# Expert lists from masks of an expert's ten usual blocks, made for five tiles at a time, with one product per choice

## The chip, the cores and the metric

One Trainium2 chip, one of its cores. The metric is the device time of one execution in microseconds; lower is better.

## The reference, cut to what matters

Attention with pooled keys gives 4608 rows of 512, a mixture of experts picks two of eight experts for each row, and a second feed-forward layer follows. The change lies in how the kernel finds the rows of each expert.

```python
x = np.ascontiguousarray(attn_out.transpose(0, 2, 1, 3)).reshape(B * S, H * D)   # 4608 x 512
...
noisy_logits = logits + noise_scale * noise
top2 = np.argpartition(-noisy_logits, 2, axis=1)[:, :2]
...
for e in range(E):                       # 8 experts
    for k in range(2):
        mask = top2[:, k] == e
        h = np.maximum(x[mask] @ w1[e], 0.0)
        out[mask] += top2_w[mask, k, None] * (h @ w2[e])
...
h = x @ w_in;  g = h - np.tanh(h);  out = g @ w_out
```

## The kernel before

The 4608 rows are 36 tiles of 128 (`NT`). The attention runs as a software pipeline of 42 steps `t`: in one step different tiles are at different stages (`st_exps`, `st_norm`, `st_attT`, `st_q`, `st_scores`, `st_x`, `st_g`, `st_av`). `st_x` makes the gate's logits on TensorE (L1147), DVE copies them (`gs`, L1150), and `st_g` of the next step multiplies that by a selector (L1161) and scales the result into `lz` (L1162). From step 36 on no new tile enters: the pipeline drains. The order on each engine is the order in which this Python program issues instructions; nothing reorders them.

The gate works on groups of 10, 10, 9 and 7 tiles. When the last tile of a group has its logits, `gate_jobs` is queued in `pend`. It is a generator: each `tick` lets it issue up to the next `yield`, and ticks are strewn over the steps, eight in a full step, so that its small DVE instructions fall between those of the attention. `yield "pe"` makes it wait for `tick_pe`, which comes once a step, at its start, and lets it issue TensorE products. A `yield` of a number holds it for so many ticks. The group's steps are: softplus of the noise, the two largest logits (`oh`, `exps`), the position of each choice in its expert's list by products with a triangular and an all-ones matrix (L1215, L1217), and then `lists`.

Position `pos` of token `128 t + lane` in expert e's list is split in block `hi = pos >> 7` and `row = pos & 127`. The list itself is the table `idx` of shape 128 x 8 x 36: `idx[row, e, block]` holds the token's number. `lists` fills it by products of masks, five tiles (`LT`) to a chunk. For every tile and choice DVE makes two row masks of 128 columns, one multiplied by the lane (L1245), one by 128 t (L1246), POOL makes a column mask of all 8 x 36 = 288 columns (L1247), and TensorE multiplies each row mask by the column mask, four products per tile, all summed in one PSUM bank (L1253). DVE adds the sum to `idx` (L1255). A chunk of five tiles is ten ticks, a `tick_pe` and an add; the eight chunks have 5, 5, 5, 5, 5, 4, 5 and 2 tiles. The bank is the one named `misc`, which L1147 and L1161 use too; in the experts' phase it is one named `pt`.

An expert usually has up to `CAP` = 1216 rows, ten blocks of 128, and the experts' phase gathers only those blocks, through `idx` (L300). If an expert has more, `overflow` (L406), a branch after the seventh expert, goes on with the blocks behind and writes them to spare rows. With the inputs here the branch is not taken.

The experts' phase goes over units `u`: a unit is one eighth of an expert's hidden layer for a group of 512, 384 or 320 rows; `L1` (L340 to L342) is its first product, with ReLU on ACT (L344) and the remainder on DVE (L345), and `L2` (L362 to L364), two units later, its second. The first four blocks of expert 0 come from the first 20 tiles alone, so the first eight units run while the gate's last two groups are still worked on: in them `gate(n)` gives ticks, and after L2 also a `tick_pe`. `run_jobs` issues conversions of weights (L237 to L242 on DVE) between those ticks. After the eighth unit's L1 all that is left of the gate is issued and blocks 4 to 6 are gathered.

POOL also sums keys and values for the attention (L1027 to L1033), issues the DMAs that add to them, and issues the gathers.

Of the kernel before, what the change touches and what calls it, by code (L numbers as in the profile page):

```python
# [10 lines left out]
F32 = mybir.dt.float32  # L11
F16 = mybir.dt.float16
BF16 = mybir.dt.bfloat16
I32 = mybir.dt.int32
AF = mybir.ActivationFunctionType
OP = mybir.AluOpType
# [7 lines left out]
QB = (-2.276397947135507, 2.3926682998872706)  # L24
TT = 0.3
CAP = 1216
SG = C4 ** 0.25
SP5 = (17 / 315) ** 0.5
NEAR0 = 1 / 3 - 17 / 315 * (21 / 17) ** 2
# [155 lines left out]
def moe(nc, tc, st, V, z):  # L185
    w_in, w_out, hold, idx, ps, W, gate = (V[n] for n in ("w_in", "w_out", "hold", "idx", "ps", "W", "gate"))
    N, E, DM, FF, F2, NT = (V[n] for n in ("N", "E", "DM", "FF", "F2", "NT"))
    identf, ones1, onec, x_d, y_d, wi, wo, cin, wn2, outc = (
        V[n] for n in ("identf", "ones1", "onec", "x_d", "y_d", "wi", "wo", "cin", "wn2", "outc"))
    wk = st.enter_context(tc.tile_pool(name="m_wk", bufs=2))  # L190
    ts = nc.vector.tensor_scalar
    tt = nc.vector.tensor_tensor
    stt = nc.vector.scalar_tensor_tensor
# [8 lines left out]
    for e in range(E):  # L202
        c = 0
# [197 lines left out]
    def norms(y, k):  # L401
        junk = wk.tile([128, DM], F32, name="qs", bufs=1)
        nc.scalar.activation(junk[:k], y[:k], AF.Square, accum_out=ystat[:k, len(done):len(done) + 1])
        done.append(k)

    def overflow():  # L406

        exps, poss, counts, cnti, ridx, tokid = (V[n] for n in ("exps", "poss", "counts", "cnti", "ridx", "tokid"))
        J0 = CAP // 128
        most = nc.values_load(cnti[:, 2 * E:2 * E + 1], min_val=0, max_val=N)  # L410
        with tc.If(most > CAP):
            small = wk.tile([128, 5, E], F32, name="small", bufs=1)
            over, used, ovb, fre = (small[:, i] for i in range(4))
            ts(used, counts, float(CAP), None, op0=OP.min)
# [10 lines left out]
            def rows(r, k, t):  # L425
                nc.vector.tensor_copy(r, k)
                for e in range(E):
# [3 lines left out]
            ef, pf = (a.rearrange("p t a o -> p (t a o)") for a in (exps, poss))  # L431
            k, r, t = (wk.tile([128, 2 * NT], F32, name=n, bufs=b)
                       for n, b in (("ca", 1), ("cb", 1), ("qs", 1)))
# [36 lines left out]
            col = small[:, 4].bitcast(I32)  # L470
# [37 lines left out]
    for e in range(E):  # L508
        if e + 1 < E:
            c1, c2 = PR[e + 1, 1], PR[e + 1, 2]  # L510
            d = 4 if e == 0 else 0
# [395 lines left out]
def attention(nc, tc, st, V):  # L907
# [88 lines left out]
    wgn = one.tile([128, HP, 32], F32, name="wgn")  # L996
    nc.vector.memset(wgn, 0.0)
    nc.vector.memset(idx, 0)
    slot = ep.tile([128, E * NT], F16, name="slot")
    nc.gpsimd.iota(slot, pattern=[[1, E * NT]], base=0, channel_multiplier=0, allow_small_or_imprecise_dtypes=True)  # L1000
    lane = ep.tile([128, 1], F32, name="lane")
    nc.gpsimd.iota(lane, pattern=[[0, 1]], base=0, channel_multiplier=1, allow_small_or_imprecise_dtypes=True)
    load_q(2)
# [8 lines left out]
    nc.gpsimd.dma_start(KV[1, "k"], kv_ap(1, "k", 0, H)[:, :, 4:8], accum_op=OP.add)  # L1012
    nc.gpsimd.dma_start(KV[1, "v"], kv_ap(1, "v", 0, H)[:, :, 4:8], accum_op=OP.add)

    zero8 = ep.tile([128, 1, E], F32, name="zero8")
    nc.vector.memset(zero8, 0.0)
    dd = ep.tile([128, NT], F32, name="dd")
# [159 lines left out]
    def gate_jobs(t0, n):  # L1177

        sl = slice(t0, t0 + n)
        g = len(tot)  # L1180
        tl = {}

        def T(nm, shp=None, d=F32):
            tl[nm] = ep.tile([128, n] + (shp or [E]), d, name="g_" + nm, bufs=1)
            return tl[nm]
        bE = [128, n, E]
        ib = iota8[:, None, :].to_broadcast(bE)
        L, Z = lz[:, sl, 0:E], lz[:, sl, E:2 * E]
        nc.scalar.activation(T("th"), Z, AF.Abs)
        nc.scalar.activation(tl["th"], tl["th"], AF.Tanh, scale=0.5)  # L1190
        yield TK
        yield ts(T("p"), tl["th"], LOG1P[-1], None, op0=OP.mult)
        for c in LOG1P[-2::-1]:
            yield stt(tl["p"], tl["p"], c, tl["th"], op0=OP.add, op1=OP.mult)
        yield stt(tl["p"], Z, 0.0, tl["p"], op0=OP.max, op1=OP.add)
        yield stt(tl["p"], tl["p"], float(np.log(2)), nz[:, sl], op0=OP.add, op1=OP.mult)
        yield tt(T("nl"), tl["p"], L, op=OP.add)
        T("oh", [2, E])
        T("ii")
        for j in range(2):  # L1200
            m, i, oh = tops[:, sl, j], exps[:, sl, j], tl["oh"][:, :, j]
            yield nc.vector.tensor_reduce(m, tl["nl"], axis=AX.X, op=OP.max)
            yield tt(tl["ii"], tl["nl"], m.to_broadcast(bE), op=OP.is_lt)
            yield stt(tl["ii"], tl["ii"], 64.0, ib, op0=OP.mult, op1=OP.add)
            yield nc.vector.tensor_reduce(i, tl["ii"], axis=AX.X, op=OP.min)
            yield tt(oh, ib, i.to_broadcast(bE), op=OP.is_equal)
            if j == 0:
                yield stt(tl["nl"], oh, -3.4e38, tl["nl"], op0=OP.mult, op1=OP.add)
        nc.scalar.activation(T("e", [2]), exps[:, sl].rearrange("p t a o -> p t (a o)"), AF.Copy, scale=float(NT))
        M = mb[g]  # L1210
        yield tt(M[:, 0:n], tl["oh"][:, :, 0], tl["oh"][:, :, 1], op=OP.add)
        yield "pe"
        p = gate_ps[-1]([128, n + 1, E])
        f = lambda a: a.rearrange("p t e -> p (t e)")
        nc.tensor.matmul(f(p), before, f(M[:, 0:n + 1]), start=True, stop=False)  # L1215
        for k in range(1, n + 1):
            nc.tensor.matmul(f(p[:, k:n + 1]), ones, f(M[:, 0:n + 1 - k]), start=False, stop=(k == n))  # L1217
        yield
        pos = ep.tile([128, 11, E], F32, name="g_pos", bufs=2)[:, 0:n + 1]
        yield tt(pos, p, tot[-1][:, None, :].to_broadcast([128, n + 1, E]) if tot else zero8.to_broadcast([128, n + 1, E]), op=OP.add)  # L1220
        tot.append(pos[:, n])
        yield tt(tl["oh"], tl["oh"], pos[:, 0:n, None, :].to_broadcast([128, n, 2, E]), op=OP.mult)
        sp = poss[:, sl]
        with nc.allow_low_precision(reason="whole numbers below 4608, one of them not zero"):
            nc.vector.tensor_reduce(sp, tl["oh"], axis=AX.X, op=OP.add)
        yield
        spf = sp.rearrange("p t a o -> p t (a o)")
        hi, row = T("hi", [2], I32), T("row", [2])
        yield ts(hi, spf, 7, None, op0=OP.logical_shift_right)
        yield stt(row, hi, -128.0, spf, op0=OP.mult, op1=OP.add)  # L1230
        yield tt(tl["e"], tl["e"], hi, op=OP.add)
        yield from lists(t0, n, row, tl["e"])

    def lists(t0, n, row, col):


        flat = idx.rearrange("p e c -> p (e c)")
        for c0 in range(0, n, LT):
            m = min(LT, n - c0)
            R = ep.tile([128, LT, 2, 2, 128], F16, name="l_row", bufs=1)  # L1240
            C = ep.tile([128, LT, 2, E * NT], F16, name="l_col", bufs=1)
            for j in range(m):
                for a in range(2):
                    r = row[:, c0 + j, a:a + 1]
                    ts(R[:, j, a, 0], slot[:, 0:128], r, lane, op0=OP.is_equal, op1=OP.mult)  # L1245
                    ts(R[:, j, a, 1], slot[:, 0:128], r, float(128 * (t0 + c0 + j)), op0=OP.is_equal, op1=OP.mult)  # L1246
                    yield nc.gpsimd.tensor_scalar(C[:, j, a], slot, col[:, c0 + j, a:a + 1], None, op0=OP.is_equal)  # L1247
            yield "pe"
            p = gate_ps[-1]([128, E * NT])
            for j in range(m):  # L1250
                for a in range(2):
                    for b in range(2):
                        nc.tensor.matmul(p, R[:, j, a, b], C[:, j, a], start=(j + a + b == 0), stop=(j == m - 1 and a + b == 2))  # L1253
            yield
            yield tt(flat, p, flat, op=OP.add)  # L1255

    LT = 5
    TK = 7
    pend = []

    held = [0]
# [102 lines left out]
            at(37 + j, c2.low, j)  # L1364
    ex = []
    for t in range(NT + 6):
        if t + 4 < NT:
            load_q(t + 4)
        if t < NT:
            st_exps(t)  # L1370
        if 0 <= t - 4 < NT:
            st_xT(t - 4)
        if 0 <= t - 6 < NT:
            st_g(t - 6)
            if t - 6 in groups:
# [87 lines left out]
```

## Time and profile before

| | us |
|---|---|
| median of 3 runs | 1906.9 (1906.23 to 1908.49) |
| the profiled execution | 1904.05 |
| its span, first to last instruction | 1902.2 |
| PE busy | 1815.4 (95%) |
| DVE busy | 1208.2 (64%) |
| ACT busy | 781.6 (41%) |
| POOL busy | 348.9 (18%) |

PE is TensorE, DVE VectorE, ACT ScalarE, POOL GpSimd, SP the queue that issues most DMAs; PEld is PE's weight load, which runs beside its products. L12 is line 12 of the kernel. A timeline's row has the start in us from the span's start, the time taken, engine, line, operation, what is written and read, how many instructions are merged, and in brackets how long the engine stood idle before and what ended that. Instructions of one engine overlap a little, so starts lie closer than the times taken. The granted clock is a share of full speed.

### The profile page before, as it was taken

What the parts mean: (1) busy time and instruction counts of PE and PEld (TensorE: products, weight loads), DVE (VectorE), ACT (ScalarE), POOL (GpSimd) and SP (SyncE); (2) the same over time, 40 slices, a digit from 0 to 9 for tenths busy, and PEclk for the clock granted to TensorE, in tenths of its full rate; (3) what the DMA queues carried; (4) which work ended last, traced back from release to release, by engine and by line L of the source; (5) the groups of instructions that cost most, each with busy time, mean ns of one, the idle gap of its engine ahead of it and who ended that gap; (6) DMA issues with size and microseconds to landing.
All of it is one profiled execution on the core that took longest, in us unless ns stands there. A gap on an engine that the chain in (4) does not pass through costs nothing. (4 is left out here: it accounts for less than half of the span.)

```text
span 1902.2 us, 26786 instructions
## 1 busy us (share of the span) xinstructions
PE 1815.4 (95%) x10028; PEld 949.4 (50%) x10028; DVE 1208.2 (64%) x2541; ACT 781.6 (41%) x1847; POOL 348.9 (18%) x309
## 2 busy tenths in 40 slices
PE   6888988999999999999999899999999999999998
PEld 4667764444545454545545454444444444444443
DVE  4778866666656656566565456565666656566654
ACT  3766741343424343343434234443434434343432
POOL 2457435330202021010101012010100001010000
PEclk7988888999999999999999999999999999999999
DMA  9978412355464545454534333121211112120100
GB/s 178 210 155 186 115 62 84 89 126 159 118 202 136 141 135 144 124 153 122 152 94 135 97 92 86 39 78 45 56 47 42 50 40 78 44 56 29 23 22 24
DMA packets 237471, 188.67 MB, mean 99 GB/s; under 512 B 164553, under 2 KB 191177, under 8 KB 237321
## 3 DMA queue, kind: packets, MB, share of 16 engines
q1 hardware_dynamic: 213816, 139.09, 27.3%
q0 software_dynamic: 22880, 47.09, 10.8%
q8 instruction: 83, 1.36, 0.3%
q10 hardware_dynamic: 624, 0.59, 0.1%
q14 instruction: 68, 0.55, 0.1%
HBM read 117.62 MB, written 41.55 MB: 84 GB/s over the span
## 5 line engine op out<-in xcount | busy, mean ns | idle before, releaser
L344 ACT ACTIVATE hT<-ph 128x512 f16<-128x512 f32 (+2 forms) x192 | 96.7, 504 | 485.4 <-PE ph L342 475.6
L340 PE MATMUL ph<-xTp,pair 128*128 128x384 f16 (+2 forms) x736 | 245.3, 333 | 10.5 <-DVE pair L157 6.5
L342 PE MATMUL ph<-xTp,pair 128*128 128x384 f16 (+2 forms) x736 | 244.9, 333 | 2.8 <-issue 2.8
L341 PE MATMUL ph<-xTp,pair 128*128 128x384 f16 (+2 forms) x736 | 244.9, 333 | 0.4 <-DVE xTp L321 0.4
L345 DVE SCALAR_TENSOR_TENSOR hT<-ph,hT 128x512 f16<-128x512 f32 (+2 forms) x192 | 110.7, 576 | 198.0 <-ACT hT L344 197.8
L832 DVE SCALAR_TENSOR_TENSOR t<-ph,cinf,hs 128x512 f32<-128x512 f32 x141 | 105.7, 750 | 202.2 <-ACT hs L831 191.1
L831 ACT ACTIVATE hs<-ph,cinf 128x512 f32<-128x512 f32 x141 | 96.4, 684 | 301.2 <-PE ph L724 301.2
L876 PE MATMUL py<-wo,gT 128*128 128x512 f16 x576 | 218.3, 379 | 0.8 <-DVE gT L825 0.8
L364 PE MATMUL py<-pair,hT 128*128 128x512 f16 x576 | 218.3, 379 | 0.3 <-DVE hT L345 0.3
L362 PE MATMUL py<-pair,hT 128*128 128x512 f16 x576 | 218.3, 379 | 0.0
L363 PE MATMUL py<-pair,hT 128*128 128x512 f16 x576 | 218.3, 379 | 0.0
L874 PE MATMUL py<-wo,gT 128*128 128x512 f16 x576 | 218.3, 379 | 0.0
L875 PE MATMUL py<-wo,gT 128*128 128x512 f16 x576 | 218.3, 379 | 0.0
L300 POOL DMA_INDIRECT xg<-x_d,idx x75 | 79.6, 1062 | 628.8 <-DVE xp L327 487.1
L722 PE MATMUL ph<-yT,wi 128*128 128x512 f16 x512 | 194.0, 379 | 0.0
L723 PE MATMUL ph<-yT,wi 128*128 128x512 f16 x512 | 194.0, 379 | 0.0
L724 PE MATMUL ph<-yT,wi 128*128 128x512 f16 x512 | 194.0, 379 | 0.0
L664 POOL DMA_INDIRECT y<-y_d,ridx x64 | 60.6, 948 | 578.5 <-DVE y L675 354.6
L340 PEld LDWEIGHTS <-pair 128*128 128x128 f16 x768 | 75.2, 98 | 82.7 <-issue 23.9
L342 PEld LDWEIGHTS <-pair 128*128 128x128 f16 x768 | 75.3, 98 | 60.7 <-issue 4.8
L341 PEld LDWEIGHTS <-pair 128*128 128x128 f16 x768 | 75.3, 98 | 57.9 <-issue 1.7
L835 ACT ACTIVATE qa<-th,bias 128x512 f32<-128x512 f32 x144 | 102.4, 711 | 1.5 <-DVE th L833 1.4
(280 smaller groups left out, 3141.9 us busy)
## 6 DMA issues: line engine op xcount, KB each, us to landing
stage<-in_moe_w SPq DMA_DIRECT2D x64, 512.0 KB
y_d<-ys SPq DMA_DIRECT2D x82, 256.0 KB
x_d<-xr SPq DMA_DIRECT2D x36, 256.0 KB
out<-o SPq DMA_DIRECT2D x36, 256.0 KB
qt<-in_q SPq DMA_DIRECT2D x32, 256.0 KB
raw<-in_moe_w_in SPq DMA_DIRECT2D x32, 256.0 KB
raw<-in_moe_w_out SPq DMA_DIRECT2D x32, 256.0 KB
kt<-in_k SPq DMA_DIRECT2D x7, 576.0 KB
```

Source lines behind the costliest of these rows:

```text
L340: nc.tensor.matmul(p[:, :nt], w[:, 0, m, s], x[:, 0, m, :nt], start=(m == 0), stop=False)
L341: nc.tensor.matmul(p[:, :nt], w[:, 0, m, s], x[:, 1, m, :nt], start=False, stop=False)
L342: nc.tensor.matmul(p[:, :nt], w[:, 1, m, s], x[:, 0, m, :nt], start=False, stop=(m == KD - 1))
L362: nc.tensor.matmul(p, h[:, 0, s], w[:, 0, f], start=(f == 0), stop=False)
L363: nc.tensor.matmul(p, h[:, 0, s], w[:, 1, f], start=False, stop=False)
L364: nc.tensor.matmul(p, h[:, 1, s], w[:, 0, f], start=False, stop=(f == KF - 1))
L722: nc.tensor.matmul(p, wi[:, 0, m, s], y[:, 0, m], start=(m == 0), stop=False)
L723: nc.tensor.matmul(p, wi[:, 0, m, s], y[:, 1, m], start=False, stop=False)
L724: nc.tensor.matmul(p, wi[:, 1, m, s], y[:, 0, m], start=False, stop=(m == self.KD - 1))
L874: nc.tensor.matmul(p, g[:, 0, s], wo[:, 0, f], start=(f == 0), stop=False)
L875: nc.tensor.matmul(p, g[:, 0, s], wo[:, 1, f], start=False, stop=False)
L876: nc.tensor.matmul(p, g[:, 1, s], wo[:, 0, f], start=False, stop=(f == KF - 1))
```

## The change

`lists` covers only the ten usual blocks of each expert (`NB` = 10, so 80 columns in place of 288) and makes its masks for a chunk of tiles at a time. DVE compares once for all column masks of a chunk (`C0`, up to 5 x 2 x 80 elements); POOL multiplies that by 128 t (`head`, a new row of constants) and ACT by the lane, into the two halves of `C`. DVE makes one plain row mask per choice, both choices of a tile in one instruction. TensorE then needs one product of 160 columns per choice, two per tile, and DVE two adds of 80 columns. Two small DVE instructions per group push choices beyond block ten out of the table. While the attention runs, the generator is held for two ticks between its products and what reads them. In `overflow`, inside the branch, the new function `rest` makes the columns of the blocks beyond ten for all tiles.

```diff
+NB = -(-CAP // 128)
...
+    def rest(poss, exps):
+        ...
+        p = ps.tile([128, 2, E, NT - NB], F32, name="pt", bufs=2)
+        for j in range(2 * NT):
+            ts(R, slot[:, 0:128], row[:, j:j + 1], None, op0=OP.is_equal)
+            ts(C[:, 0:L], slot, col[:, j:j + 1], lane, op0=OP.is_equal, op1=OP.mult)
+            ts(C[:, L:2 * L], slot, col[:, j:j + 1], float(128 * (j // 2)), op0=OP.is_equal, op1=OP.mult)
+            nc.tensor.matmul(p.rearrange("p x e c -> p (x e c)"), R, C, start=(j == 0), stop=(j == 2 * NT - 1))
+        d = idx[:, :, NB:NT]
+        nc.vector.tensor_copy(d, p[:, 0])
+        tt(d, p[:, 1], d, op=OP.add)
...
         with tc.If(most > CAP):
+            rest(poss, exps)
...
-    slot = ep.tile([128, E * NT], F16, name="slot")
-    nc.gpsimd.iota(slot, pattern=[[1, E * NT]], ...)
+    slot = ep.tile([128, 128], F16, name="slot")
+    nc.gpsimd.iota(slot, pattern=[[1, 128]], ...)
...
+    head = ep.tile([128, NT], F32, name="head")
+    nc.gpsimd.iota(head, pattern=[[128, NT]], ...)
...
-        nc.scalar.activation(T("e", [2]), exps[:, sl]..., AF.Copy, scale=float(NT))
+        nc.scalar.activation(T("e", [2]), exps[:, sl]..., AF.Copy, scale=float(NB))
...
-        yield
+        yield 2 * (now[0] < NT)
...
         yield tt(tl["e"], tl["e"], hi, op=OP.add)
+        over = T("ov", [2])
+        yield ts(over, hi, float(NB), 1000.0, op0=OP.is_ge, op1=OP.mult)
+        yield tt(tl["e"], tl["e"], over, op=OP.add)
         yield from lists(t0, n, row, tl["e"])
...
     def lists(t0, n, row, col):
-        flat = idx.rearrange("p e c -> p (e c)")
+        K = E * NB
+        flat = idx[:, :, 0:NB]
         for c0 in range(0, n, LT):
             m = min(LT, n - c0)
-            R = ep.tile([128, LT, 2, 2, 128], F16, name="l_row", bufs=1)
-            C = ep.tile([128, LT, 2, E * NT], F16, name="l_col", bufs=1)
+            R = ep.tile([128, LT, 2, 128], F16, name="l_row", bufs=1)[:, 0:m]
+            C0 = ep.tile([128, LT, 2, K], F16, name="l_one", bufs=1)[:, 0:m]
+            C = ep.tile([128, LT, 2, 2, K], F16, name="l_col", bufs=1)[:, 0:m]
+            b = lambda a, k: a[:, c0:c0 + m, :, None].to_broadcast([128, m, 2, k])
+            w = lambda k: slot[:, None, None, 0:k].to_broadcast([128, m, 2, k])
+            yield tt(C0, w(K), b(col, K), op=OP.is_equal)
+            nc.gpsimd.tensor_tensor(C[:, :, :, 1], C0, head[:, t0 + c0:t0 + c0 + m, None, None].to_broadcast([128, m, 2, K]),
+                                    op=OP.mult)
+            yield nc.scalar.activation(C[:, :, :, 0], C0, AF.Copy, scale=lane)
+            for j in range(m):
+                yield tt(R[:, j], w(128)[:, j], b(row, 128)[:, j], op=OP.is_equal)
+            yield "pe"
+            p = gate_ps[-1]([128, 2, E, NB])
             for j in range(m):
                 for a in range(2):
-                    r = row[:, c0 + j, a:a + 1]
-                    ts(R[:, j, a, 0], slot[:, 0:128], r, lane, op0=OP.is_equal, op1=OP.mult)
-                    ts(R[:, j, a, 1], slot[:, 0:128], r, float(128 * (t0 + c0 + j)), op0=OP.is_equal, op1=OP.mult)
-                    yield nc.gpsimd.tensor_scalar(C[:, j, a], slot, col[:, c0 + j, a:a + 1], None, op0=OP.is_equal)
-            ...
-                        nc.tensor.matmul(p, R[:, j, a, b], C[:, j, a], ...)
-            yield
-            yield tt(flat, p, flat, op=OP.add)
+                    nc.tensor.matmul(p.rearrange("p x e c -> p (x e c)"), R[:, j, a], C[:, j, a].rearrange("p x k -> p (x k)"),
+                                     start=(j + a == 0), stop=(j == m - 1 and a == 1))
+            yield 2 * (now[0] < NT)
+            yield tt(flat, p[:, 0], flat, op=OP.add)
+            yield tt(flat, p[:, 1], flat, op=OP.add)
...
     for t in range(NT + 6):
+        now[0] = t
```

## Rows read from the trace of the kernel before

**Rows 1.** Busy time by stretch: PE, PEld, DVE, ACT, POOL (instructions); clock, DMA share, GB/s

```profile
154.00:198.50 44.50, 37.67 (x376) 31.56 (x375) 36.97 (x110) 27.73 (x121) 33.88 (x28) 0.92 0.91 198
...
224.00:262.00 38.00, 33.90 (x317) 27.42 (x316) 27.40 (x101) 23.45 (x103) 21.84 (x20) 0.87 0.16 50
...
262.00:297.00 35.00, 28.82 (x239) 21.20 (x238) 22.76 (x81) 11.98 (x20) 14.54 (x15) 0.71 0.28 91
...
297.00:352.00 55.00, 50.96 (x247) 24.15 (x248) 36.26 (x134) 7.57 (x14) 25.61 (x25) 0.94 0.24 77
...
352.00:1902.20 1550.20, 1522.98 (x7613) 731.77 (x7611) 953.01 (x1780) 601.42 (x1097) 180.69 (x173) 1.00 0.33 91
```

**Rows 2.** Groups by shape, 0 to 420 us: busy, mean ns, idle before

```profile
L1247 POOL TENSOR_SCALAR l_col<-slot,g_e 128x288 f16<-128x288 f16 x72 | 77.1, 1198 | 62.7 <-DVE g_e L1231 51.1 <-PE misc L1253 10.8 <-PE pt L1253 0.9
```

**Rows 3.** Timeline of DVE, 150 to 262 us, line L1111

```profile
154.15 0.75 DVE L1111 TENSOR_TENSOR at<-at,rc 128x576 f32<-128x576 f32 x1
...
198.49 0.76 DVE L1111 TENSOR_TENSOR at<-at,rc 128x576 f32<-128x576 f32 x1
...
209.12 0.75 DVE L1111 TENSOR_TENSOR at<-at,rc 128x576 f32<-128x576 f32 x1
...
224.09 0.75 DVE L1111 TENSOR_TENSOR at<-at,rc 128x576 f32<-128x576 f32 x1
...
261.91 0.76 DVE L1111 TENSOR_TENSOR at<-at,rc 128x576 f32<-128x576 f32 x1
```

**Rows 4.** Waits of PE, 150 to 297 us: total, times, longest

```profile
PE misc L1161 <- DVE gs L1150: 10.7, 7, 3.6
```

**Rows 5.** Timeline of PE and one stretch, attention steps and drain

```profile
204.02 0.61 PE L1161 MATMUL misc<-sel,gs 128*128 128x16 f32 x2 [1.73 <-DVE gs L1150]
...
204.00:210.00 6.00, 5.75 (x31) 4.90 (x31) 6.00 (x12) 1.99 (x6) 3.61 (x2) 0.50 0.24 57
...
243.30 2.62 PE L1253 MATMUL misc<-l_col,l_row 128*128 128x288 f16 x20
...
291.66 4.64 PE L1253 MATMUL misc<-l_col,l_row 128*128 128x288 f16 x20 [1.32 <-DVE lz L1162]
```

**Rows 6.** Timelines of PE, POOL and DVE and one stretch, first expert units

```profile
326.07 0.90 PE L1253 MATMUL pt<-l_col,l_row 128*128 128x288 f16 x6
...
333.66 0.63 PE L340 MATMUL ph<-x0T,pair 128*128 128x512 f16 x1
...
323.06 10.12 POOL L1247 TENSOR_SCALAR l_col<-slot,g_e 128x288 f16<-128x288 f16 x10 [18.76 <-DVE g_e L1231]
...
329.88 0.68 DVE L345 SCALAR_TENSOR_TENSOR hT<-ph,hT 128x512 f16<-128x512 f32 x1
...
326.00:337.00 11.00, 7.86 (x31) 3.44 (x29) 7.61 (x30) 0.00 (x0) 10.14 (x11) 0.69 0.13 43
```

**Rows 7.** Timeline of DVE, first and last row mask of one chunk

```profile
284.05 0.31 DVE L1245 TENSOR_SCALAR l_row<-slot,g_row,lane 128x128 f16<-128x128 f16 x1
...
288.80 0.24 DVE L1246 TENSOR_SCALAR l_row<-slot,g_row 128x128 f16<-128x128 f16 x1
```

**Rows 8.** Groups by shape that give prices: busy, mean ns

```profile
L1222 DVE TENSOR_TENSOR g_oh<-g_oh,g_pos 128x160 f32<-128x160 f32 x2 | 0.6, 324 | 0.0
...
L1220 DVE TENSOR_TENSOR g_pos<-misc,g_pos 128x88 f32<-128x88 f32 x1 | 0.2, 249 | 0.5 <-PE misc L1217 0.5
...
L152 ACT ACTIVATE pair<-stage,wsc 128x1024 f16<-128x1024 f32 x12 | 13.5, 1139 | 2.6 <-DVE wsc L140 2.6
```

**Rows 9.** Timelines of POOL and DVE at 200 us

```profile
199.74 2.59 POOL L1027 TENSOR_TENSOR kt<-kt 72x1024 f32<-72x1024 f32 x1 [7.94 <-PE psc L1088]
...
202.40 1.26 POOL L1028 TENSOR_TENSOR kc<-kt 72x512 f32<-72x512 f32 x1
...
200.39 2.03 DVE L1194 SCALAR_TENSOR_TENSOR g_p<-g_p,g_th 128x80 f32<-128x80 f32 x1
```

**Rows 10.** Instructions of line L411 on PE: duration ns

```profile
L411 PEldq COMPARE_BRANCH  x1: 4017/4017/4017, 1045.4 to 1045.4; - x1
```

More of the change, by code (lines that the diff above doesn't have):

```diff
@@ L404, in norms @@
         done.append(k)
+    def rest(poss, exps):
+        T = wk.tile([128, 4, 512], F32, name="qf", bufs=1)
+        pf, ef = (a.rearrange("p t a o -> p (t a o)") for a in (poss, exps))
+        L = E * (NT - NB)
+        hi, row, col, lane = T[:, 0, 0:2 * NT].bitcast(I32), T[:, 0, 128:128 + 2 * NT], T[:, 0, 256:256 + 2 * NT], T[:, 0, 400:401]
+        g = nc.gpsimd.iota
+        slot = T[:, 1].bitcast(F16)[:, 0:L]
+        R = T[:, 2].bitcast(F16)[:, 0:128]
+        C = T[:, 3].bitcast(F16)[:, 0:2 * L]
+        g(slot, pattern=[[1, L]], base=0, channel_multiplier=0, allow_small_or_imprecise_dtypes=True)
+        g(lane, pattern=[[0, 1]], base=0, channel_multiplier=1, allow_small_or_imprecise_dtypes=True)
+        ts(hi, pf, 7, None, op0=OP.logical_shift_right)
+        stt(row, hi, -128.0, pf, op0=OP.mult, op1=OP.add)
+        stt(col, ef, float(NT - NB), hi, op0=OP.mult, op1=OP.add)
+        ts(col, col, float(-NB), None, op0=OP.add)
+        u = T[:, 2, 128:128 + 2 * NT]
+        ts(u, hi, float(NB), -1000.0, op0=OP.is_lt, op1=OP.mult)
+        tt(col, col, u, op=OP.add)
+        p = ps.tile([128, 2, E, NT - NB], F32, name="pt", bufs=2)
[7 more added lines that the diff above has]
+        tt(d, p[:, 1], d, op=OP.add)
     def overflow():
@@ L998, in attention @@
     nc.vector.memset(idx, 0)
-    slot = ep.tile([128, E * NT], F16, name="slot")
-    nc.gpsimd.iota(slot, pattern=[[1, E * NT]], base=0, channel_multiplier=0, allow_small_or_imprecise_dtypes=True)
+    slot = ep.tile([128, 128], F16, name="slot")
+    nc.gpsimd.iota(slot, pattern=[[1, 128]], base=0, channel_multiplier=0, allow_small_or_imprecise_dtypes=True)
     lane = ep.tile([128, 1], F32, name="lane")
@@ L1013, in attention @@
     nc.gpsimd.dma_start(KV[1, "v"], kv_ap(1, "v", 0, H)[:, :, 4:8], accum_op=OP.add)
+    head = ep.tile([128, NT], F32, name="head")
+    nc.gpsimd.iota(head, pattern=[[128, NT]], base=0, channel_multiplier=0, allow_small_or_imprecise_dtypes=True)
     zero8 = ep.tile([128, 1, E], F32, name="zero8")
@@ L1208, in gate_jobs @@
                 yield stt(tl["nl"], oh, -3.4e38, tl["nl"], op0=OP.mult, op1=OP.add)
-        nc.scalar.activation(T("e", [2]), exps[:, sl].rearrange("p t a o -> p t (a o)"), AF.Copy, scale=float(NT))
+        nc.scalar.activation(T("e", [2]), exps[:, sl].rearrange("p t a o -> p t (a o)"), AF.Copy, scale=float(NB))
         M = mb[g]
@@ L1242, in lists @@
             for j in range(m):
                 for a in range(2):
-                    r = row[:, c0 + j, a:a + 1]
-                    ts(R[:, j, a, 0], slot[:, 0:128], r, lane, op0=OP.is_equal, op1=OP.mult)
-                    ts(R[:, j, a, 1], slot[:, 0:128], r, float(128 * (t0 + c0 + j)), op0=OP.is_equal, op1=OP.mult)
-                    yield nc.gpsimd.tensor_scalar(C[:, j, a], slot, col[:, c0 + j, a:a + 1], None, op0=OP.is_equal)
-            yield "pe"
-            p = gate_ps[-1]([128, E * NT])
@@ L1250, in lists @@
[L1250 to L1253, printed above, removed]
-            yield
-            yield tt(flat, p, flat, op=OP.add)
+                    nc.tensor.matmul(p.rearrange("p x e c -> p (x e c)"), R[:, j, a], C[:, j, a].rearrange("p x k -> p (x k)"),
+                                     start=(j + a == 0), stop=(j == m - 1 and a == 1))
@@ L1257, in attention @@
+            yield 2 * (now[0] < NT)
+            yield tt(flat, p[:, 0], flat, op=OP.add)
+            yield tt(flat, p[:, 1], flat, op=OP.add)
     LT = 5
     TK = 7
+    now = [0]
     pend = []
```

## Prediction

> **What bounds the kernel now.** I read the busy time by stretch first [rows 1]. From 352 us to the end TensorE is busy 1523 of 1550 us at the full clock, and the change touches nothing there except code that is jumped over, so its gain or loss lies ahead of 352. Ahead of it three stretches have the change's lines in them. In the attention steps (154 to 262, first and second group of tiles) PE is busy about nine tenths, but at a granted clock of 0.92 and 0.87: it is often late rather than full. In the drain of the pipeline (262 to 297) the clock is 0.71. From 297 the experts have begun and PE is the bound again, 51 of 55 us, at 0.94.
>
> The groups of instructions by shape then give the size of the thing changed [rows 2]: POOL spends 77 us on 72 column masks; each of the 36 tiles has four list products of 288 columns on PE, 144 in all.
>
> The starts of the attention normalisation (L1111) give the pace of a step [rows 3]. Three steps without list work go from 209.12 to 224.09, 5.0 us each. The six from 154.15 to 198.49, with the first group's lists and the tail of its gate work, take 44.3, 14 more than six quiet ones; the five from 224.09 to 261.91, with the second group's, take 37.8, 13 more than five. That excess of 27 us is the most the lists can cost there.
>
> What ends last in those steps is told by PE's waits: seven for DVE's gs copy, 10.7 us [rows 4]. PE's timeline shows the rest [rows 5]: a chunk's 20 products take 2.62 us at full clock and 4.64 at half clock (drain), and around a wait of 1.73 us the clock is 0.50, the lower of its two levels (1.2 of 2.4 GHz), from 204 to 210. So DVE's lateness is paid twice.
>
> In the experts' stretch the reader is to see one place [rows 6]: PE reaches the last group's first chunk at 326.07 and can go on with expert work only at 333.66, 7.6 us for products worth 2.62, because POOL's ten masks for it run from 323.06 to 333.2. DVE was back at expert work (L345) at 329.88. The clock from 326 to 337 is 0.69.
>
> **The change part by part.** *PE.* Of a chunk of five tiles, 20 products of 288 columns become 10 of 160. By the row 2.62/20 = 0.131 each; if a product goes with its columns, 0.073 each; if by its weight load or a fixed cost, at most 0.131. Ten cost 0.73 to 1.31; I take 0.9, near the columns, since the 288 columns show no gap between products. Four chunks fall in attention steps, where PE is the engine that does them while DVE waits for the sum: 4 x 1.7 = 6.9 us (5.2 to 7.6). Two smaller chunks are done at full clock amid expert work, 16 products to 8 and 8 to 4: 12 products fewer and the other 12 shorter, 24 x 0.131 - 12 x 0.09 = 2.1 us (1.5 to 2.3). The one in the drain at half clock goes from 4.64 to about 1.5, 3.2 us; but PE's unbroken work there is also what precedes the clock's return, and shorter, it leaves some first expert products at half speed. I give back 1.4 for that, add 0.5 for DVE: 2.3 us (1 to 4).
>
> *DVE.* Ten pairs of row masks and some small work go from 284.05 to 289.04 [rows 7], so about 0.47 us a pair start to start, 4.7 a chunk, and 0.4 for the add into idx. Now a chunk has one comparison of 800 elements, five of 256, and two adds of 80. Between 160 elements (0.32) [rows 8] and 576 (0.75) [rows 3] a comparison costs 1.03 ns an element more: 0.98 and 0.42 us, start to start some 0.07 less. An add of 88 elements from PSUM is 0.25 [rows 8]. So 0.9 + 5 x 0.35 + 2 x 0.2, with the two new small ops of each group 3.2 us for 5.1. That 1.9 us is a gain only as far as POOL doesn't hold DVE up.
>
> *POOL.* Ten masks become one product of 800 elements of two operands. The nearest row of its kind, two operands, is 1.26 us for 512, so 2.0; the dearest by element is the mask it replaces (1198 ns for 288), so 3.3. I take 2.0, the likest operation. It waits for the mask comparison; behind it stand key and value sums, which stood behind ten masks before. It can hold DVE up: at 200.39 a DVE instruction of 80 elements (88 take 0.25 [rows 8]) took 2.03 us, until the POOL sum begun at 199.74 was over [rows 9]. The new row comparisons have two SBUF operands as that one had. A row comparison usually comes one to three DVE instructions behind the mask comparison, so part of POOL's 2.0 us passes under PSUM copies; I take 1.0 us lost a chunk (0 to 2.0 or 3.3). The Trainium skill states the same as a rule (SBUF — State Buffer, "SBUF: two separate sides"): the port pair that GpSimd and VectorE share is locked for a whole instruction, and the loser blocks fully. By it the loss would be the whole 2.0 us wherever a comparison stands right behind, and DVE's gain would be nothing. That is the second rival below.
>
> So DVE gains 0.9 us a chunk where it is the last. What counts is the stalls it causes. Of the 10.7 us of waits for gs I take 2.5 as going, with one loss of clock less, some 2.5 us of half speed (half of the 5 to 6 us of one such stretch): 5.0 us (0 to 12, all waits gone and one drop).
>
> *ACT* gets eight copies of up to 800 elements, at most 1.14 us (that is 1024) [rows 8]. It is 17 us idle of 44.5 in the first stretch [rows 1], and the copy falls behind a comparison issued one tick earlier, so it hides; if it doesn't, xr waits up to 1 us and the list products up to 1 us, four times.
>
> *The place at 326.* POOL's chain of 10.1 us becomes a comparison (0.98 + 0.34 for the two new small ops) and a 2.0 us product, from 323.06 to about 326.4, off the path. DVE is now last: it had ten pairs and a six-instruction conversion up to 329.88, now the pairs' 4.7 us are 2.9 of comparisons and 0.3 of small ops, so it ends near 328.4, or 330.4 if POOL's product is added whole. PE goes on at 329 instead of 333.66: 4.5 us (2.5 if DVE is blocked, 6.8 if nothing waits, 8 if the clock stays up as well). Of the half clock behind it I count nothing.
>
> *What costs nothing.* The hold of two ticks before each sum, and the second add, delay idx by a few DVE instructions; by counting the ticks the products are issued at the same steps as before (steps 23, 25, 33, 35, 41, units 2, 5 and 6), and what reads idx (the first gathers) is issued behind both kernels' same step. The misc bank is held longer, but its next writer comes after the scores. The head iota is one small POOL instruction at the start. The overflow branch has some 290 more instructions, jumped over: PE's branch there takes 4.0 us today [rows 10]; I price the longer body at nothing, at most another such 4.0.
>
> **Sum.** 6.9 + 5.0 (attention) + 2.3 (drain) + 2.1 + 4.5 (experts) = 20.8 us. Profiled execution: 1904.05 with a span of 1902.2, becomes 1883.3 and a span of about 1881.4. It lay 2.9 us under the median of the runs, 1906.9; the same gain from that median gives **1886**. Low ends: 5.2 + 0 + 1 + 1.5 + 2.5 = 10 us, 1897; high ends: 7.6 + 12 + 4 + 2.3 + 8 = 34, 1873.
>
> **The rivals.** *Attention keeps its pace.* From 154 to 198.5 the DMA share is 0.91 [rows 1], and steps may wait for loads as soon as they wait less for DVE. Then the first two terms shrink to 1 or nothing, and 2.3 + 2.1 + 4.5 = 9 remains, 5 if the drain gives nothing: 1898 to 1902. Against it: the view of [rows 4] names no load, and the share is 0.16 in the second group's steps.
>
> *POOL's product holds DVE (slower).* At 199.74 two POOL sums, 3.85 us together, precede PE's 1.73 us wait and 6 us at half clock; that step took 10.63 us instead of 5.0, 5.6 lost. At 2.0 to 3.3 us the new product would lose 2.9 to 4.8 in each of five chunks (four in attention, one in the drain), at worst 24, against the 6.9 + 2.3 + 2.1 + 2.5 = 13.8 that then are left: 10 slower, 1917. It decides from 2.8 us lost per chunk on. For it: the row. Against it: DVE is busy all of 204 to 210 [rows 5] with POOL on for only 3.6 us of it, so other work helped to fill that step; and the old masks kept POOL busy five times as long.
>
> *The stalls vanish altogether.* List steps fall to near the quiet pace, the clock stays up: 28 to 36 us, 1871 to 1879. For it: 27 us of excess; against: gate arithmetic and key preparation are in the excess too.
>
> **How the numbers follow.** Forecast (10 to 28 us) 0.60, attention keeps its pace 0.18, stalls vanish 0.09, held up so that little is left (within 0.2%, 3.8 us, which is about what a measurement of this kernel can tell from none) 0.07, slower 0.06. Faster 0.60 + 0.18 + 0.09 = 0.87, same 0.07, slower 0.06. The range, 1872 to 1902, takes in the forecast's bounds, most of the first rival and of the third.
>
> **What would show it.** Right: POOL's list work near 15 us instead of 77; 72 list products of some 0.08 us start to start; the steps of 224 to 262 five or so us shorter; the wait at 326 down to some 3 us; everything behind 352 moved as one. Wrong: row comparisons of 1 to 2.5 us while POOL multiplies, PE's waits for gs above 10.7 us, a clock below 0.87 in the attention steps, a new wait of ACT for the mask comparison, or waits for q loads in steps 20 to 26.

## The result, and the profile after

The changed kernel takes 1881.4 us (median of 4 runs, 1878.25 to 1882.34) beside 1907.0 for the kernel before (1906.23 to 1908.49): a ratio of 0.9859, 95% interval 0.9841 to 0.9877, 25.6 us faster. Run again later (e10), it came to 0.9857 (0.9836 to 0.9877). The forecast was 1886, range 1872 to 1902. The profiled execution took 1880.52 us with a span of 1878.7.

In the trace the line numbers have moved: L1111 is L1144, the gs copy L1150 is L1183, the expert products L340 are L341, and the list work stands at L1282 (comparison of 800), L1283 (POOL's product), L1285 (ACT's copy), L1287 (row comparison), L1292 (list products), L1295 and L1296 (adds into idx).

The groups by shape, 0 to 420 us, of the changed kernel, against [rows 2]:

```profile
L1287 DVE TENSOR_TENSOR l_row<-slot,g_row 128x256 f16<-128x256 f16 x36 | 21.1, 608 | 0.0
...
L1283 POOL TENSOR_TENSOR l_col<-l_one,head 128x800 f16<-128x800 f16 x6 | 9.3, 1544 | 65.9 <-DVE l_one L1282 54.5 <-PE pt L1187 11.4
L1282 DVE TENSOR_TENSOR l_one<-slot,g_e 128x800 f16<-128x800 f16 x6 | 6.6, 1108 | 0.2
```

With the two shorter chunks (1.3 and 0.7 us) POOL's list work is 11.3 us in place of 77.1.

The timeline of DVE at the same steps as in [rows 3], and busy time from the start of one normalisation to that of another (columns as in [rows 1]; the last row is the drain, up to the first expert product):

```profile
158.93 0.76 DVE L1144 TENSOR_TENSOR at<-at,rc 128x576 f32<-128x576 f32 x1
...
197.78 0.76 DVE L1144 TENSOR_TENSOR at<-at,rc 128x576 f32<-128x576 f32 x1
...
225.34 0.76 DVE L1144 TENSOR_TENSOR at<-at,rc 128x576 f32<-128x576 f32 x1
...
253.21 0.76 DVE L1144 TENSOR_TENSOR at<-at,rc 128x576 f32<-128x576 f32 x1
```

```profile
158.93:197.78 38.85, 33.51 (x366) 27.65 (x362) 34.80 (x86) 29.24 (x127) 16.96 (x10) 0.96 1.00 220
...
225.34:253.21 27.87, 25.65 (x297) 21.19 (x294) 24.70 (x75) 22.81 (x98) 3.05 (x2) 1.00 0.21 64
...
258.70:285.44 26.74, 20.41 (x189) 15.26 (x188) 20.01 (x61) 11.06 (x18) 3.96 (x4) 0.80 0.29 94
```

The first group's six steps take 38.9 us (44.3 before), the second group's five 27.9 (37.8), at the full clock. The quiet steps between became 2.0 us longer, and the step behind 253.21 takes 5.5 in place of 3.4. The drain is 26.7 (31.6). The reader should see one more thing: before any list work the changed kernel is 4.8 us *later* (158.93 against 154.15). That isn't the change: among all traces of this study the same step starts between 154.2 and 163.8, in both kinds of kernel. So stages are compared, not times of day.

PE's waits from 154 to 300 us (total, times, longest), against [rows 4]; the second row is the wait for a q load at 177.86 us:

```profile
PE misc L1194 <- DVE gs L1183: 7.3, 5, 4.5
...
PE pt L1111 <- DMA qt<-in_q: 1.1, 1, 1.1
...
PE misc L1180 <- DVE idx L1296: 1.0, 1, 1.0
```

One chunk's products, against the 2.62 us of [rows 5], and the place of [rows 6], by the timelines of PE, DVE and POOL:

```profile
241.41 0.87 PE L1292 MATMUL misc<-l_col,l_row 128*128 128x160 f16 x10
...
314.52 0.38 PE L365 MATMUL py<-pair,hT 128*128 128x512 f16 x1
316.21 1.65 PE L1292 MATMUL pt<-l_col,l_row 128*128 128x160 f16 x10 [1.31 <-DVE l_row L1287]
317.70 0.38 PE L341 MATMUL ph<-x0T,pair 128*128 128x512 f16 x1
...
313.21 1.61 DVE L240 TENSOR_SCALAR ca<-ca 128x256 f32<-128x256 f32 x1
...
313.06 1.61 POOL L1283 TENSOR_TENSOR l_col<-l_one,head 128x800 f16<-128x800 f16 x1 [25.59 <-DVE l_one L1282]
```

PE is away from expert work from 314.90 to 317.70, 2.8 us in place of 7.6, and DVE is what it waits for. Why DVE is late stands in the last two rows: the conversion L240 took 1.61 us while POOL's product ran, where the nine others up to 420 us took 0.27 to 0.29. In e8 and e11 (below), without that product, the conversion ahead of this chunk takes 0.28 and 0.29 us and PE doesn't wait for the row masks.

Behind 337 us, where the forecast had everything move as one, another 5.1 us came: 2.1 on the way to the overflow branch and 3.0 behind the jump. The kernel before has this row of PE's timeline there, on which no engine or transfer is named, and the changed kernel has no such stall (its branch on PE takes 3657 ns for the 4017 of [rows 10]):

```profile
1054.40 0.39 PE L342 MATMUL ph<-xTp,pair 128*128 128x512 f16 x1 [2.81 <-issue]
```

**Stages of all traces.** In us: start of the twentieth normalisation; from there to the first expert product on x0T; from that to the first on xTp (first expert's units); to the first product behind the jump; to the start of PE's last product. (e1 to e12 are described below.)

| kernel | step 20 at | attention, drain | units | to the jump | behind it |
|---|---|---|---|---|---|
| before | 154.2 | 142.8 | 58.1 | 694.6 | 845.6 |
| e2 before, long body | 158.6 | 144.8 | 58.8 | 694.0 | 844.8 |
| e9 before, filled body | 157.3 | 144.4 | 58.9 | 693.7 | 842.7 |
| e7 products of 80 | 159.6 | 136.9 | 58.8 | 693.8 | 844.3 |
| e6 masks of 80 | 156.9 | 131.6 | 52.2 | 694.5 | 844.3 |
| e3 both of 80 | 158.6 | 123.4 | 52.4 | 695.6 | 846.9 |
| e5 e3, long body | 157.4 | 126.5 | 51.9 | 694.1 | 844.4 |
| e4 late groups only | 155.4 | 138.3 | 52.1 | 692.1 | 842.7 |
| after | 158.9 | 126.5 | 51.4 | 692.5 | 842.7 |
| e10 after again | 155.3 | 127.6 | 51.6 | 693.4 | 842.7 |
| e1 after, short body | 157.6 | 127.7 | 51.6 | 691.9 | 842.7 |
| e8, e11 product on ACT | 155.4, 158.9 | 125.2, 125.8 | 50.3, 49.8 | 693.0, 693.4 | 842.7, 842.8 |
| e12 product on DVE | 163.8 | 124.9 | 49.5 | 691.8 | 842.7 |

Whole executions spread more (the kernel before from 1901.3 to 1916.1 us beside e1 to e12). Between like kernels the attention column and the one up to the jump repeat within some 3 us, the units within 1; behind the jump, kernels without the stall lie at 842.7 or at 844.3 to 844.8. By them the changed kernel gains 16.3 + 6.7 + 2.1 + 3.0 us and starts 4.8 late: 23.3 us of PE's last product (1895.35 to 1872.02).

### The profile page after: what moved, and what is told of

Its sections match the earlier page's. It is cut to its first block, busy times and chain, and to the rows that moved or that the text cites. A ratio compares the mean times of both kernels' runs of the same rounds, so it can differ in the third digit from the quotient of the medians.

```text
span 1878.7 us, 26520 instructions
## 1 busy us (share of the span) xinstructions
PE 1797.7 (96%) x9956; PEld 937.0 (50%) x9956; DVE 1207.2 (64%) x2457; ACT 787.0 (42%) x1855; POOL 285.2 (15%) x246
## 5 line engine op out<-in xcount | busy, mean ns | idle before, releaser
L341 PE MATMUL ph<-xTp,pair 128*128 128x384 f16 (+2 forms) x736 | 245.3, 333 | 9.9 <-DVE pair L158 6.3
L341 PEld LDWEIGHTS <-pair 128*128 128x128 f16 x768 | 75.1, 98 | 82.3 <-issue 23.3
```

What stands on the lines that cost most here:

```text
L341: nc.tensor.matmul(p[:, :nt], w[:, 0, m, s], x[:, 0, m, :nt], start=(m == 0), stop=False)
```

## The experiments

**e1 and e2: the overflow body.** In e1 the changed kernel loses the call, in e2 the kernel before gets it, with the function:

```diff
         with tc.If(most > CAP):
-            rest(poss, exps)
```

> The changed kernel without the new code of the overflow branch (with these inputs the branch is jumped over, so the output is the same; a list overflow would lose columns). What is open: behind 337 us the changed trace gains another 5.1 us, 3.4 of them at the branch itself (PE idle 1.16 + 2.81 us before, 0.80 after, COMPARE_BRANCH 4017 against 3657 ns). Theory A, the longer body is what made the jump cheaper: without it about 3.4 us come back, 1884.8 us. Theory B, the jump is cheaper because PE and the other engines arrive at it in another order, whatever stands in the body: 1881.4 us, within 0.8. Theory C, the body costs something of its own: below 1880.5.

> The kernel before with the new code added to its overflow branch and nothing else; the branch is jumped over with these inputs. Theory A (the longer body makes the jump cheaper): 1906.9 - 3.4 = 1903.5 us. Theory B (the order of arrival does): 1906.9, within 0.8. Theory C (the body costs): above 1907.7, at most 4 us more.

e1: 1881.3 us, ratio 0.9869 (0.9846 to 0.9892); no stall. e2: 1905.6, ratio 0.9983 (0.9968 to 0.9998); the 2.81 us are gone from its trace. Neither simple theory holds: the long body removes the stall in the kernel before, and the changed kernel has none without it either.

**e3: 80 columns alone.** The structure of before, narrowed, with the two small DVE instructions per group that the changed kernel has too (the diff is shortened):

```diff
-C = ep.tile([128, LT, 2, E * NT], F16, name="l_col", bufs=1)
+C = ep.tile([128, LT, 2, K], F16, name="l_col", bufs=1)   # K = E * NB = 80
-nc.gpsimd.tensor_scalar(C[:, j, a], slot, col[...], None, op0=OP.is_equal)
+nc.gpsimd.tensor_scalar(C[:, j, a], slot[:, 0:K], col[...], None, op0=OP.is_equal)
-nc.tensor.matmul(p, R[:, j, a, b], C[:, j, a], ...)          # 288 columns
+nc.tensor.matmul(p.rearrange("p e c -> p (e c)"), R[:, j, a, b], C[:, j, a], ...)
```

A later block of a list, which these inputs don't have, is left out of it.

> The kernel before with 80 columns in place of 288 in its masks and products (two small operations per group are added to push a later block out of range) and with its structure kept: POOL's masks one by one, DVE's pairs of row masks, four products a tile. Theory 1 (fewer columns give PE's part and POOL's at 326, the rest of the gain needs the work that left DVE): 20 products of 80 columns take about 1.6 us in place of 2.62, so 1.0 x 4 in attention, some 1.6 in the drain, 1.2 amid expert work, and at 326 DVE's ten pairs (to 329.9) set the end in place of POOL's masks (333.2), 3.5: together 10 us, 1897 us (1893 to 1901). Theory 2 (the width alone does it, DVE's work is hidden): 20 us or more, 1887 or less. Theory 3 (a POOL mask has a fixed cost, 80 columns cost nearly the 1.2 us of 288): no gain at 326, 1900 to 1903.

1885.2 us, ratio 0.9879 (0.9858 to 0.9900). Theory 1 was mine and it fell, and theory 2 stands: with no row mask less, no product merged and no column mask joined, the attention and drain are as short as in the changed kernel (123.4 us beside 126.5 to 127.7) and the units within 1 us. Its chunk of 20 products of 80 columns takes 0.9 us at full clock, not the 1.6 that I expected. What e3 lacks is behind the jump. From its timeline of PE:

```profile
1034.11 0.38 PE L342 MATMUL ph<-xTp,pair 128*128 128x512 f16 x1 [2.43 <-issue]
1034.32 0.46 PE L343 MATMUL ph<-xTp,pair 128*128 128x512 f16 x1
1034.58 0.63 PE L341 MATMUL ph<-xTp,pair 128*128 128x512 f16 x1
```

The unexplained stall is there, and then products of 0.63 us in place of 0.38 up to 1037.95: the lower clock costs another 1.7.

**e4: new lists for groups 2 and 3 only**, old ones of 288 columns for the two groups in the attention steps (`g >= 2` chooses):

> New lists for groups 2 and 3 only (one chunk in the drain, three amid expert work), the old ones of 288 columns for groups 0 and 1 in the attention steps; the longer overflow body is in. Theory 1, the gains add by place: the first expert units' 6.7 us, the drain's own part of the 11.5 that the trace shows ahead of the first expert product (2.3 to 4.9), and up to 5.1 behind 337: 1906.9 - 14 to 17 = 1890 to 1893 us. Theory 2, what is gained in attention is the cause of what is gained later (the clock at the drain, the order of DVE's work): only the place at 326 and its products remain, 1900 us.

1892.5 us, ratio 0.9921 (0.9904 to 0.9937). Theory 1: the attention steps are those of before (44.6 and 36.9 us), the drain gains 2.8, the units 6.0, and 5.5 come behind them. The gains add by place, as theory 1 has it (1890 to 1893).

**e5: e3 with the long body.** e3 and the added lines of e2.

> The kernel of e3 (the kernel before with masks and products of 80 columns, four products a tile, DVE's pairs and POOL's masks one by one) with the new code added to its overflow branch, which is jumped over. Theory 1 (the whole gain is the 80 columns and the place of the code behind the jump; merging the products and taking work off DVE give nothing): e3 lost 2.43 us without a waiting reason seven products behind the jump and some 1.6 at half clock after it; both go, 1885.2 - 4 = 1881 us, ratio 0.986, that of the full change. Theory 2 (the merging has a worth of its own of 3 us or more): the stall behind the jump stays or is made good elsewhere, 1884 us or more.

1883.5 us, ratio 0.9862 (0.9838 to 0.9886), no stall behind the jump: the changed kernel's ratio to within 0.0003, though the interval is 4.6 us to either side. In microseconds it lies 2.5 above theory 1's 1881 and 0.5 under theory 2's bound, beside a kernel before that took 1909.4 in these runs. So merging the products and taking work off DVE show no worth of their own, but one of up to some 4 us isn't ruled out.

**e6 and e7: which of the two widths.** Both with the long body. In e6 POOL writes 80 columns of a mask that was zeroed at the start and PE streams all 288; in e7 POOL makes 288 and PE streams 80 (shortened):

```diff
 e6
+tensor_scalar(C[:, j, a, 0:K], slot[:, 0:K], ...)
+matmul(p, R[:, j, a, b], C[:, j, a], ...)
 e7
+tensor_scalar(C[:, j, a], slot, ...)
+matmul(p, R[:, j, a, b], C[:, j, a, 0:K], ...)
```

> As e5, but only the masks are narrow: POOL writes 80 columns into a mask buffer of 288 that is zeroed once at the start, and each product still streams 288 columns. Theory POOL (what matters is that POOL is done with a chunk sooner: masks of 0.50 in place of 1.00 us): the place at 326 (3.5 us) and whatever POOL held up in attention, half of e3's 20.7 us or more: 1890 us or less. Theory PE (what matters is the time of the products): only the place at 326 and the branch, 1908 - 3.5 - 3.5 = 1900 us.

> As e5, but only the products are narrow: POOL's masks keep 288 columns, the products stream the first 80. Theory PE: 20 products go from 2.62 to some 1.8 us at full clock (0.09 each, as the 160 columns of the changed kernel took), so 0.8 x 4 in attention, 1.0 amid expert work, 1 to 3 in the drain, 3.5 of the branch: 9 to 11 us, 1897 to 1899; if the clock and the stalls hang on the products, up to 20, 1888. Theory POOL: with POOL's masks as before, 3.2 + 1 + 3.5 at most, 1900 us.

e6: 1891.8 us, ratio 0.9918 (0.9895 to 0.9941), 2 us above the bound of theory POOL and 8 under theory PE. e7: 1899.3, 0.9946 (0.9927 to 0.9965), which lies between the numbers of its two theories. POOL's part is the larger one. By stages the masks alone give 11.2 us in attention and drain and all of the 6 in the units; the products alone give 5.9 and nothing in the units. From the twentieth normalisation to the last, the thirty-sixth, the split is plainest (starts of L1111 and its counterparts, 154.15 to 265.32 in the kernel before): 111.2 us before, 102.5 in e6, 105.8 in e7, 97.8 with both (e5). e7's 5.4 is no more than its products became shorter (four chunks of 20, each 0.89 us at full clock where it was 2.62); e6's 8.7 holds no product time at all. How a mask on POOL can cost time on other engines stands in two views. e6's groups by shape (the row masks are DVE's, unchanged in its code):

```profile
L1285 POOL TENSOR_SCALAR l_col<-slot,g_e 128x80 f16<-128x80 f16 x72 | 38.3, 555 | 58.0 <-DVE g_e L1268 30.3 <-PE pt L1167 19.7 <-PE misc L1291 8.0
L1283 DVE TENSOR_SCALAR l_row<-slot,g_row,lane 128x128 f16<-128x128 f16 x72 | 23.2, 323 | 0.0
```

and the same groups of e7:

```profile
L1282 POOL TENSOR_SCALAR l_col<-slot,g_e 128x288 f16<-128x288 f16 x72 | 77.3, 1096 | 45.9 <-DVE g_e L1265 23.7 <-PE pt L1164 17.9 <-PE misc L1288 3.9
L1280 DVE TENSOR_SCALAR l_row<-slot,g_row,lane 128x128 f16<-128x128 f16 x72 | 30.9, 437 | 0.0
```

DVE's 72 row masks by the lane take 437 ns while POOL makes wide masks (427 in the kernel before) and 323 while it makes narrow ones: 7.7 us of DVE came back without these instructions being touched. The means hide two things. In the drain and the units most of these masks are longer (median 0.42 us before, 0.31 in e6); in the attention steps the median is nearly the same (0.31 and 0.30) and a few long ones make the mean, the longest 1.49 us at 175.37 under a value sum of POOL's (L1032). That DVE's rows are the path from POOL's masks to the step is argued, not isolated: over the eleven list steps DVE is busy 64.0 us before, 64.0 in e7 and 56.9 in e6, which fits, but POOL's key and value sums, which stand behind its masks, are another path that no run separates. In the units PE keeps POOL's pace. e7's timeline of PE:

```profile
331.76 0.29 PE L1288 MATMUL pt<-l_col,l_row 128*128 128x80 f16 x2 [0.74 <-POOL l_col L1282]
332.74 0.29 PE L1288 MATMUL pt<-l_col,l_row 128*128 128x80 f16 x2 [0.68 <-POOL l_col L1282]
333.72 0.29 PE L1288 MATMUL pt<-l_col,l_row 128*128 128x80 f16 x2 [0.68 <-POOL l_col L1282]
```

Products of a quarter of the columns come 0.98 us apart, a mask's length, as those of 288 did.

The second group's steps show the clock. Busy time of the kernel before, of e6 and of e7 over the same five steps:

```profile
224.09:261.91 37.82, 33.72 (x316) 27.24 (x314) 27.22 (x100) 23.36 (x102) 21.84 (x20) 0.86 0.16 50
```

```profile
224.79:255.97 31.18, 29.29 (x317) 24.03 (x315) 24.35 (x102) 23.11 (x102) 10.79 (x20) 1.00 0.20 61
```

```profile
227.67:259.38 31.71, 27.97 (x314) 23.45 (x312) 26.18 (x102) 23.11 (x102) 22.28 (x20) 0.90 0.18 55
```

PE runs the same instructions in the first two (a record more in e6). 33.72 at 0.86 is about 29.0 at full clock, so 4.4 of e6's 6.6 us are half-speed time that didn't come, and 2.2 idle time. e7 takes 6.1 us off these steps, 3.5 of them by its products; its clock is 0.90, and in the step behind them it falls to 0.50, where 2.6 us are lost again.

**e8, e11 and e12: where the new product of 800 elements runs.** In e8 and, once more, in e11 ACT makes it, five copies with a constant scale; in e12 DVE does:

```diff
-nc.gpsimd.tensor_tensor(C[:, :, :, 1], C0, head[...], op=OP.mult)
+for j in range(m):                                              # e8, e11
+    nc.scalar.activation(C[:, j, :, 1], C0[:, j], AF.Copy, scale=float(128 * (t0 + c0 + j)))
+yield nc.vector.tensor_tensor(C[:, :, :, 1], C0, head[...], op=OP.mult)   # e12
```

> The changed kernel with the block column (the one-hot times 128 times the tile's number) made by ACT, five copies of 160 elements with a constant scale, in place of POOL's one product of 800 elements. POOL then has no list work at all. Theory lock (row comparisons of 1.0 to 1.6 us behind POOL's product, in place of 0.41, delay the list products): 0.6 to 1.2 us in each of four attention chunks and the place at 316, 2 to 5 us faster: 1876 to 1879. Theory hidden (DVE's wait for POOL passes under other work): 1881.4 within 0.8. Theory ACT (1.6 us more on ACT per chunk delays x and what follows): 1 to 5 us slower.

> The changed kernel itself once more, beside e11 and e12 on the same chip: 1878 to 1884 us, ratio 0.986; from the start of the step with the first list work (the twentieth normalisation of attention) to the first expert product 126 to 128 us, as in its first trace and in e1 (126.5, 127.7).

> e8 once more, since its executions spread over 20 us. Theory lock (POOL's product costs something by holding the row comparisons): 2 to 5 us faster than e10, and once more no wait of TensorE for row masks in the first expert units (1.31 us in the changed kernel, none in e8). Theory hidden: within 1 us of e10.

> The changed kernel with the product of 800 elements on DVE in place of POOL. DVE pays for it itself, some 1.0 us a chunk by the row of its comparison of 800 (0.98), and gets back the 0.6 to 1.2 us that its row comparisons lose behind POOL's. Theory lock (DVE loses as much behind POOL as the product would cost it): within 1.5 us of e10. Theory cover (POOL does the product beside DVE and the hold costs little): 1 us in each of four attention chunks and the place at 316, 3 to 6 us slower.

e8: 1882.7 us, 0.9880 (0.9845 to 0.9915). e10, the changed kernel: 1880.0, 0.9857. e11: 1881.4, 0.9878 (0.9852 to 0.9904). e12: 1880.2, 0.9850 (0.9831 to 0.9869). No place of the product is told from another by the times. The traces show the hold at one spot: the units take 1.1 to 2.1 us less without POOL (49.5 to 50.3 against 51.4 to 51.6). For e8 and e11 I had expected 2 to 5 us: a miss. e12, 0.2 us from e10, lies where theory lock put it. No version of this study beats the changed kernel by more than the runs can tell.

**e9: a body of products.** The kernel before with 72 products of TensorE, never run, in the branch that is jumped over:

```diff
         with tc.If(most > CAP):
+            p = ps.tile([128, 512], F32, name="pt", bufs=2)
+            for j in range(72):
+                nc.tensor.matmul(p[:, 0:128], identf, identf, start=(j == 0), stop=(j == 71))
```

> The kernel before with 72 products of TensorE put into its overflow branch and nothing else; the branch is jumped over, so none of them runs. Theory place (the 2.8 us without a reason, eight products behind the jump, are PE waiting for a piece of its instructions that is fetched only then; where the pieces begin hangs on the number of instructions ahead): the shift moves the piece's edge, the stall at that product is gone or lies at another product, 82 or 83 pieces on the instruction queue accordingly, and the kernel is at most 3.4 us faster, 1903 to 1908 beside a kernel before at 1907 to 1909. Theory content (it was the index arithmetic of the new body on DVE and GpSimd that mattered in e2 and e5): the stall stays at 2.8 us and the eighth product.

1905.2 us, ratio 0.9984 (0.9968 to 0.9999). The stall is gone, and PE is done 842.7 us behind the jump, as in the changed kernel. The DMA queues' view (packets, MB, share) of e9 has

```profile
q8 instruction: 82, 1.34, 0.3%
```

and that of the kernel before

```profile
q8 instruction: 83, 1.36, 0.3%
```

The two kernels with the stall, before and e3, are the two with 83 packets on this queue; the others have 82. In both, one of them moves in the microsecond in which the stall begins (1051 to 1052; 1031 to 1032 in e3). A packet close behind the jump is no sign by itself: the changed kernel has one at 1030.4, 1.1 us behind its jump, and no stall.

## Why the prediction was right, point by point

**Attention.** Forecast 6.9 for the products and 5.0 for stalls, 11.9. Measured: 5.5 and 9.95 us in the list steps, less 2.0 in the quiet steps and 2.1 in the step behind 253.21, 11.4. Ten products take 0.87 us at full clock where twenty took 2.62, so that term is 7.0 and 4.4 are left for the stalls. In the second group's steps about 3.4 us are products, 1.9 idle time, and 4.7 the clock (33.72 us at 0.86 became 25.65 at 1.00).

**The step that failed** is the one that named the source of the 5.0 us: DVE's fewer instructions, 1.9 us less a chunk. e3 and e5 keep every row mask and lose the stalls all the same; e6, with row masks and products as they were, gains 8.7 us in these steps by POOL's narrower column masks. The prediction gave POOL a role only at 326 and as the danger of the new product. It counted the masks' 77 us as harmless in attention, and the row that spoke against it was in the profile unread: row masks of 0.43 us mean where one of [rows 7] took 0.31. Joining the masks, the four products made two and the offload of the row products moved nothing that these runs can tell (e5), so the part of the change that is hard to write shows no worth beside the width. That 11.4 came so near to 11.9 is therefore luck for the part of the stalls: the 5.0 was a guess within 0 to 12, its source was another, and the sum is right in size alone.

**The wait that was said not to come.** PE's 1.0 us for idx at L1296, where the next writer of the misc bank stood behind the held second add; the prediction had the scores before it. It is half of what the step behind 253.21 gives back.

**The drain.** Forecast 2.3, measured 4.9: I gave back 1.4 for clock lost, and the clock rose to 0.80 (0.68 before over the same steps). Some of that may be chance: e2 and e9 have the old lists and a clock of 0.83 there, and take 30.2 and 30.1 us where the kernel before took 31.6.

**The units.** Forecast 2.1 for products and 4.5 for the place, 6.6; measured 6.7. The wait of 2.8 us was forecast at 3. But the split is off, and that the two came to 6.6 is luck too: e6 gets 6.0 with wide products, and e5 only 0.3 more with narrow ones. Nor did POOL's masks alone hold PE at 326: PE's waits of 297 to 352 us in the kernel before give them 1.6 us and the row masks 1.5.

```profile
PE pt L1253 <- POOL l_col L1247: 1.6, 4, 0.6
PE pt L1253 <- DVE l_row L1246: 1.2, 2, 0.6
...
PE pt L1253 <- DVE l_row L1245: 0.3, 1, 0.3
```

**POOL's new product.** 2.0 us forecast, 1.54 measured. A row comparison that is free takes 0.41 us; the mean of 36 is 0.608, so 7.1 us over the eight chunks, 0.9 each where 1.0 was forecast. By the Trainium skill (SBUF — State Buffer, "SBUF: two separate sides") the loser waits for the whole instruction; that agrees here: at 233.42, under a product from 232.71 to 234.23, a comparison took 1.09 us. For the old masks the trace differs: at 1.00 us each, ten in a row, they made a row mask only 0.1 us longer than the narrow ones did (427 against 323 ns in the mean) and did not stop it. The rival built on the rule did not come about: e8, e11 and e12 remove POOL's product and gain at most the 2 us in the units, where the held conversion L240 is the wait that can be seen.

**The signs.** Of the signs of being right, POOL's list work (11.3 us), the length of a product (0.09 us) and the wait at 326 (2.8 us) came; the steps of the second group became 10 us shorter, twice what was named. Of the signs of being wrong three came as well and meant little: row comparisons of 1.0 to 2.4 us behind POOL (six of the 36), ACT waiting 15.8 us in six waits for the mask comparison (150 to 345 us), and 1.1 us of waiting for one q load. Waits for gs above 10.7 us and a clock below 0.87, the signs nearest to PE, did not come (7.3 us; 0.96 and 1.00).

**Behind 352** the forecast was that all moves as one. 3.0 us behind the jump go with the place of the code: the new body (e2) and 72 idle products (e9) each remove the stall from the kernel before, and the changed kernel without the body (e1) has none. That the stall is a late fetch of instructions fits the 83rd packet; the packet was not moved by itself, so this stays unproven. Of the 2.1 us ahead of the jump 1.7 are one wait of PE for DVE's `cm` (L128) at 406.29 us, which this trace of the changed kernel lacks; e10, the same kernel, has it with 1.2 us (693.4 beside 692.5), so I don't count it as the change's. Of the kernels whose stall is gone, e2, e5, e6 and e7 are still 1.6 to 2.1 us longer behind the jump than the rest; in e5 ACT waits 5.4 us for a transposing transfer (L722, 1113.10) where it waits 3.6 in the changed kernel, and PE 1.9 us behind that. Why is open.

In sum the forecast was 4.6 us too high. By the traces the attention came 0.5 us short of its terms, the drain 2.6 and the units 0.1 above theirs, and 3.0 (the place of the code) and 2.1 came behind, where nothing was forecast; 4.8 went to the later start: 23.3 us in the traces, 25.6 in the medians.

## What to carry to other kernels

Look at an elementwise engine's mean against its shortest row before calling a neighbour's work hidden. POOL's 77 us of masks hardly show in PE's list of waits (0.3 us up to 297, 1.6 behind it), and narrowing them alone still gave e6 the larger part of the gain: at the first units by PE's waits, in attention, as it seems, through DVE's longer rows and then TensorE's clock. When a change has several parts, try the cheapest first: here 80 columns in place of 288 gave the time, and the restructuring came out even, as far as runs that differ by some 4 us can tell. A few microseconds that appear behind a jump far from the change are to be tested with an idle body of code before they are counted.

## What the runs showed of the hardware that was not expected

- A POOL mask of 80 columns takes 0.50 us at the median (e3) and one of 288 takes 1.00 (the kernel before); a line through these two is 0.31 us and 2.4 ns a column.
- A POOL product of two operands, 800 elements, takes 1.52 us, 1.9 ns an element, where the f32 sum of 512 in [rows 9] took 2.5.
- Where POOL's product of two operands ran, DVE was held also in an instruction with a single input: the conversion L240 took 1.61 us in place of 0.28 (1.61 and 1.62 in e10 and e1 as well).
- Code that never runs moved PE by 3 us: with 72 skipped products (e9) a stall of 2.81 us eight products behind the jump was gone; in e3 such a stall also brought the lower clock for the products that followed it.
